# Three chained layers: the fifth attention tile's place in the order, and the weight steps and first split of the last slab

## The chip, the cores and the metric

The kernel runs on one core of a Trainium2 chip. The metric is the device time of one execution in microseconds (us), as the median of several runs. The engines are TensorE (PE, matmuls and transposes), VectorE (DVE), ScalarE (ACT), GpSimd (POOL) and SyncE (SP), which issues the DMAs. Each engine takes its own list of instructions in order.

## The reference

Three layers in a row, on 8 sequences of 576 tokens. Attention over chunks of 64 (8 heads of 64), a layer norm and a feed-forward block of 512 to 2048 to 512 with a residual, and a gated block with a convolution over 3 tokens:

```python
attn = softmax(q_c @ k_c.T / sqrt(64)) @ v_c          # per chunk of 64 tokens and head
x = attn, heads side by side                          # 4608 tokens x 512
xn = (x - mean(x)) / sqrt(var(x) + 1e-6) * g_ln
x2 = x + relu(xn @ w_ch1) @ w_ch2
h = relu(x2 @ w_in)
c = conv3(h, conv_w)                                  # per channel, over 3 tokens of the sequence
out = (h / (1 + exp(-c))) @ w_out
```

## The kernel before

**Precision.** Every fp32 matmul is three passes (L114 to L116, `mm3`): both operands are split in a high and a low part, high by a ScalarE copy, low by a VectorE subtraction. The weights arrive as 64-bit numbers. Turning a piece of 128 x 512 into fp32 takes a step of ScalarE (a, L134) and three of VectorE (t, m and n: L140, L146, L152); for w_ch1 a scaling by g_ln (g), sums (s), and the high and low parts (h, l) come after.

**Stages.** The 4608 tokens are 36 tiles T of 128, and 9 slabs p of 512. In the first stage, for each slab, x @ w_ch1 is computed by a scheme of Strassen's kind: 7 products per quarter G of the columns, 28 slots per slab. A product is 12 matmuls 128x256; its operands are sums of weight blocks and of token blocks (j, u, v make them for a slab). Products 1, 6, 7 and 4 are copied from their bank in PSUM by ScalarE (u1, u6, u7 and u4, L606 and L615), VectorE adds, and the result goes to `hd` in DRAM. Blocks 0 and 1 of the weights (pieces 0 to 7) are the first half of the columns (G = 0, 1), blocks 2 and 3 (pieces 8 to 15) the second. Next is the down phase: for each slab 16 pieces f, each 12 matmuls 128x512. `hr` is reloaded from `hd`, `split` makes hh (ScalarE, relu) and hl (VectorE), `down` multiplies by w_ch2. Then comes the gate phase (w_in, convolution, tanh, w_out).

**Attention inside the first stage.** A tile T has the steps L (load of q, k, v), S (scores on TensorE), M (maximum, VectorE), E (8 exponentials, ScalarE), R (reciprocals, VectorE), P (transposes, TensorE), C (copy, ScalarE), V (values, TensorE), X (scaling on VectorE, store of xd), B (statistics), y (xn), z (transposes), e (copy to bst). What runs ahead of slab 0 is written by hand in the table START: one step after another, W0 to W15 being loads of weight pieces and L0 to L5 of tiles. Behind the bar come lists for slots 0, 1, 2, ... of slab 0, divided by "/"; each list is run after the product of its slot. Later tiles come in by `session(t, tv)`: V of tile tv, S and M of tile tv + 1, X and the load of tile tv + 2 at slot t, halves of E at t + 1 and t + 2, R, P and C at t + 4. The sessions 4 to 7 have slots of their own in slab 0. All loads and stores go by SyncE's queue, in the order of issue; x has two buffers (`bufs=2`), so the third X waits for the first store of xd.

**The last slab.** In slab 8 the pieces of w_ch2 are brought in by a pipeline: `cv_load(n)` issues n loads, and one `cv_step()` runs a of one piece, the VectorE steps of the next older one, and the high and low parts of older ones, then loads one more. The first pieces (`F_ORDER[:4]`, tiles wd0 to wd3) go to the pool `dp` from slot (0,5) on; at (2,5) the other 12 are loaded into tiles of the first half's weights, which are free by then. At (3,2) the two first `hr` are loaded. The split of the first f (`parts = down.split(f)` at n == 0) comes behind all of the slab's products:

```python
for n, (p, f) in enumerate(todo):
    if n == 0:
        parts = down.split(f)
    hh, hl = parts
```

**Between down and gate.** The residual sum x2 (xr, L160) is transposed into the tile x2T (L762, two buffers) and stored in `x2d` (L763), four times for each slab. In the loops these four stand at every second f; those of the last slab are run in a row, behind the last matmuls. The gate tiles (i, f) follow on bank 4 + f % 4: matmuls, relu on ScalarE (hb, L882), taps on VectorE (L897), tanh on ScalarE, gt on VectorE.

Of the kernel before, what the change touches and what calls it, by code (L numbers as in the profile page):

```python
# [8 lines left out]
F32 = mybir.dt.float32  # L9
# [6 lines left out]


START = """
W0 W2 L0 W1 W3 L1 W4 W6 W5 L2 W7 L3 W8 W10 L4 W9 W11 W12 W14 W13 W15 L5
a0 t0 m0 n0 a2 t2 g0 m2 h0 n2 l0 g2 S0 M0 a1 t1 E0 m1 n1 t3 a3 P0 R0 g1  # L20
m3 C0 n3 S1 h1 g3 l1 V0 M1 h2 a4 l2 E1 X0 s0 t4 s2 a6 P1 s1 a5 t5 h4 s3
C1 m5 h3 l4 V1 m4 S2 l3 t6 h5 R1 m6 a7 t7 M2 X1 E2 n5 S3 B1 B0 g5 P2 R2
C2 M3 V2 y0 E3 n6 z0 y1 m7 n4 g6 P3 R3 n7 e0 X2 C3 z1 g7 l5 V3 e1 B2 h9
S4 X3 u1 h8 s4 g4 M4 h6 s6 h7 s5 E4 l6 s7 B3 h11 P4 y2 C4 l11 z2 y3 e2 l7
z3 v1 e3 l9 l8 u3 j0 u2 h10 v3 u5 v2 l10 v5 h12 j1 l12 u7 j2 h13 v7 u6 j3 l13
u4 v6 v4 R4
|
a8 t8 a10 t10 m8 n8
/ g8 a9 t9 m10 n10
/ g10 a11 a12 t11 t12 m9  # L30
/ a14 n9 t14 g9 m12
/ h14 n12 m11 g12 n11 a13
/ l14 t13 g11 m14 h15
/ n14 s8 g14 l15 a15
# [11 lines left out]
def attn_moe_moe2(  # L46
# [34 lines left out]
    NF1 = w_ch1.shape[1] // 128  # L81
# [131 lines left out]
    def cv_load(n=1):  # L213
        for _ in range(n):
            if pieces:
                p = pieces.pop(0)()
                p.load()
                stages[0].append(p)

    def cv_step():  # L220

        now = [s.pop(0) if s else None for s in stages]
        if now[2]:
            now[2].h()
        if now[0]:
            now[0].a()
        if now[1]:
            now[1].m()
        if now[3]:
            now[3].l()  # L230
        for s, p in zip(stages[1:], now):
            if p:
                s.append(p)
        cv_load()
# [21 lines left out]
    def add_w2(f, pool, tag):  # L256
        add(rows(w_ch2, f), w2, f, pool, tag)
# [261 lines left out]
    with tc.manual_schedule():  # L519
# [145 lines left out]
        for tv in range(4, NTILE):  # L665

            t = 28 * (tv // 4 - 1) + 7 * (tv % 4 - 1) + 1
            session({4: 1, 5: 8, 6: 12, 7: 16}.get(tv, t), tv)

        class Down:  # L670

# [21 lines left out]
            def down(self, f, hh, hl):  # L693
                for i in range(4):
                    s = slice(i * 128, (i + 1) * 128)
                    mm3(self.acc[i], hh[:, s], hl[:, s], w2[f][:, 0, :], w2[f][:, 1, :],
                        f == 0, f == NF1 - 1)

        F_ORDER = [f + 8 * i for f in range(8) for i in range(2)]
        dp = None  # L700
        for p in range(NS + 1):
            if p + 1 < NS:
                slabs[p + 1] = Slab(p + 1)
            for G in range(4):
                for s, (n, lag) in enumerate(SLOTS):
                    t = 28 * p + 7 * G + s
                    pp, GG = (p, G - lag) if G >= lag else (p - 1, 3)
                    if 0 <= pp < NS:
                        product(pp, GG, n)
                        nxt = slabs.get(pp + 1)  # L710
                        if GG == 3 and nxt:
                            if n == 1:
                                nxt.j(0)
                                nxt.j(1)
                            nxt.both(n)
                    for fn in events.pop(t, ()):
                        fn()
                    if p == 0 and t < len(later):
                        for step in later[t]:
                            one(step)  # L720
                    if p == NS - 1:
                        if (G, s) == (0, 5):
                            at.p.release()
                            dp = tc.alloc_tile_pool(name="dp", bufs=1, reuse_waits="tile")
                            for i, f in enumerate(F_ORDER[:4]):
                                add_w2(f, lambda: dp, f"wd{i}")
                            cv_load(2)
                        elif (G, s) == (2, 5):
                            tags = [f"w0{kk}{i}" for kk in range(2) for i in range(7)]
                            for f, tag in zip(F_ORDER[4:], tags):  # L730
                                add_w2(f, lambda: wa_p, tag)
                            cv_load(12)
                        elif (G, s) > (0, 5) and s % 2 == 0:
                            cv_step()
                        if (G, s) == (3, 2):
                            down = Down(0)
                            for f in range(2):
                                down.load(f)


        su_p.release()
# [14 lines left out]
        def finish(down, xr):  # L756
            for i in range(4):
                plus(xr[i], down.acc[i], xr[i])
            for i in range(4):
                def store(T=down.T[i], x=xr[i]):  # L760
                    x2T = dp.tile([128, 512], F32, tag="x2T", bufs=2, name="x2T")
                    nc.vector.transpose(out=x2T, in_=x)  # L762
                    nc.sync.dma_start(out=x2d[T].rearrange("p g t -> p (g t)"), in_=x2T)  # L763
                late.append(store)
# [24 lines left out]
        xb = [x_parts(pbx, "xb0")]  # L789
        todo = [(p, f) for p in range(NS) for f in F_ORDER]  # L790
        downs = {0: down}
        xrs = {}
        for n, (p, f) in enumerate(todo):
            if n == 0:
                parts = down.split(f)
            hh, hl = parts

            if f < 8:
                ahead = p * 8 + f + 2
                if ahead < 8 * NS:  # L800
                    if ahead % 8 == 0:
                        downs[ahead // 8] = Down(ahead // 8)
                    downs[ahead // 8].load(ahead % 8)
            if n + 1 < len(todo):
                parts = downs[todo[n + 1][0]].split(todo[n + 1][1])
            if p == 0 and n % 4 < 3 or n % 2:
                cv_step()
            if f == 4:
                xrs[p] = residual(downs[p])
            if late and f >= 8:  # L810
                late.pop(0)()
            downs[p].down(f, hh, hl)
            if f == NF1 - 1:
                finish(downs[p], xrs[p])
            if (p, f) == (0, 15):
                cv_rest()
                load_cw()
                wb_tags = [(wb_p, f"w1{kk}{i}") for kk in range(2) for i in range(7)]
                wb_tags += [(pbx, "wx0"), (pbx, "wx1")]
                for i in range(16):  # L820
                    pool, tag = wb_tags[i]
                    if i < 8:
                        add_wi(i // 4, i % 4, lambda pool=pool: pool, tag)
                    else:
                        add_wo(i - 8, lambda pool=pool: pool, tag)
                cv_load(4)
            if (p, f) == (6, 0):
                load_x2(0)
            if p == 6 and f in (8, 9, 10, 11):
                split_x2(0, f - 8)  # L830
# [182 lines left out]
```

## Time and profile before

| | before |
|---|---|
| median of 3 runs | 1318.85 us (1318.01 to 1320.35) |
| profiled execution, own time | 1322.7 us |
| its span | 1320.8 us |
| TensorE busy | 1247.7 us (94%) |
| VectorE busy | 749.0 us (57%) |
| ScalarE busy | 615.6 us (47%) |
| matmuls | 9096 |

The chain of work that ended last is 88% TensorE, 5% DMA and 4% VectorE. The page gives the span in 40 slices of 33 us: TensorE's busy share is low in the first three or four slices and once again in the fifteenth and sixteenth, the passage from the first stage to the down phase; else it is over 90%. A row of a timeline has the start, the duration, the engine, the line, the operation and the tile, and in brackets for how long the engine had been idle ahead of it and what it waited for.

### The profile page before, as it was taken

What the parts mean: (1) busy time and instruction counts of PE and PEld (TensorE: products, weight loads), DVE (VectorE), ACT (ScalarE), POOL (GpSimd) and SP (SyncE); (2) the same over time, 40 slices, a digit from 0 to 9 for tenths busy, and PEclk for the clock granted to TensorE, in tenths of its full rate; (3) what the DMA queues carried; (4) which work ended last, traced back from release to release, by engine and by line L of the source; (5) the groups of instructions that cost most, each with busy time, mean ns of one, the idle gap of its engine ahead of it and who ended that gap; (6) DMA issues with size and microseconds to landing.
All of it is one profiled execution on the core that took longest, in us unless ns stands there. A gap on an engine that the chain in (4) does not pass through costs nothing.

```text
span 1320.8 us, 23297 instructions
## 1 busy us (share of the span) xinstructions
PE 1247.7 (94%) x9096; PEld 1088.2 (82%) x9096; DVE 749.0 (57%) x1430; ACT 615.6 (47%) x1510; POOL 75.1 (6%) x172
## 2 busy tenths in 40 slices
PE   5468999999999996999999999999999999999998
PEld 4367999999999995787888888888888888888887
DVE  6597565565566455757743333433886555655550
ACT  6575565555565443433422223222675555555541
POOL 0000000000000000000000000000121111111000
PEclk6588999999999998999999999999999999999999
DMA  9523555545554348376543456443111011101001
GB/s 259 171 87 123 192 184 176 178 172 190 185 186 166 131 160 326 120 236 231 196 159 120 149 178 196 132 135 112 48 57 56 25 56 57 56 25 56 25 24 48
DMA packets 127021, 177.70 MB, mean 135 GB/s; under 512 B 12736, under 2 KB 72128, under 8 KB 126912
## 3 DMA queue, kind: packets, MB, share of 16 engines
q1 hardware_dynamic: 126912, 176.22, 40.2%
q8 instruction: 71, 1.16, 0.4%
q14 instruction: 38, 0.31, 0.1%
HBM read 110.13 MB, written 66.06 MB: 133 GB/s over the span
## 4 chain that ended last, share of the span: by engine, by line
PE 88%; DMA 5%; DVE 4%; ACT 2%; SPq 0%; issue 0%; POOL 0%; DVEq 0%; ACTq 0%; POOLq 0%
PE banks L114 28%; PE banks L115 27%; PE banks L116 27%; DMA w<-in_moe_w_ch_dram 2%; PE banks L381 2%; PE banks L463 1%; DMA rq<-in_q_dram 1%; PE banks L421 1%; DVE w L157 1%; DMA hr<-hd 1%; DMA xd<-x 1%; DMA wd<-in_moe_w_ch_dram 0%; DVE xr L160 0%; ACT pp L407 0%; ACT w L336 0%
## 5 line engine op out<-in xcount | busy, mean ns | idle before, releaser
L114 PE MATMUL banks<-xc,w 128*128 128x256 f32 x1008 | 289.9, 288 | 6.6 <-ACT u L606 5.8
L115 PE MATMUL banks<-xc,w 128*128 128x256 f32 x1008 | 282.6, 280 | 0.6 <-DVE xc L157 0.6
L116 PE MATMUL banks<-xc,w 128*128 128x256 f32 x1008 | 282.1, 280 | 0.0
L686 ACT ACTIVATE hh<-hr 128x512 fp32r<-128x512 f32 x144 | 90.9, 632 | 279.0 <-PE banks L116 269.5
L687 DVE SCALAR_TENSOR_TENSOR hl<-hr,hh 128x512 fp32r<-128x512 f32 x144 | 99.2, 690 | 204.9 <-ACT hh L686 204.9
L114 PEld LDWEIGHTS banks<-xc,w 128*128 128x128 f32 x1008 | 192.5, 191 | 10.0 <-ACT u L606 6.5
L115 PEld LDWEIGHTS banks<-xc,w 128*128 128x128 f32 x1008 | 192.9, 191 | 0.8 <-DVE xc L157 0.8
L116 PEld LDWEIGHTS banks<-xc,w 128*128 128x128 f32 x1008 | 192.7, 191 | 0.0
L114 PE MATMUL banks<-w,hl 128*128 128x512 f32 x432 | 168.5, 390 | 0.0
L115 PE MATMUL banks<-w,hh 128*128 128x512 f32 x432 | 168.1, 389 | 0.0
L116 PE MATMUL banks<-w,hh 128*128 128x512 f32 x432 | 168.1, 389 | 0.0
L897 DVE SCALAR_TENSOR_TENSOR cv<-hb,cw_sb,cv 128x510 f32<-128x510 f32 (+31 forms) x256 | 117.3, 513 | 0.6
L115 PE MATMUL banks<-xb,w 128*128 128x512 f32 x288 | 113.0, 392 | 0.0
L114 PE MATMUL banks<-xb,w 128*128 128x512 f32 x288 | 112.9, 392 | 0.0
L116 PE MATMUL banks<-xb,w 128*128 128x512 f32 x288 | 112.8, 392 | 0.0
L160 DVE TENSOR_TENSOR u<-banks,u 128x512 f32<-128x512 f32 x108 | 73.6, 689 | 60.0 <-ACT u L606 32.8
L114 PEld LDWEIGHTS banks<-w,hl 128*128 128x128 f32 x432 | 81.1, 188 | 18.3 <-DVE hl L687 1.4
L116 PEld LDWEIGHTS banks<-w,hh 128*128 128x128 f32 x432 | 81.1, 188 | 17.0
L115 PEld LDWEIGHTS banks<-w,hh 128*128 128x128 f32 x432 | 81.1, 188 | 16.5
L606 ACT COPY u<-banks 128x512 f32<-128x512 f32 x108 | 64.0, 593 | 59.9 <-PE banks L116 56.8
L407 ACT ACTIVATE pp<-banks,mx 128x64 f32<-128x64 f32 x288 | 87.7, 333 | 3.3 <-DVE mx L398 2.8
L115 PE MATMUL banks<-w,Gh 128*128 128x512 f32 x216 | 84.3, 390 | 0.0
(106 smaller groups left out, 2095.0 us busy)
## 6 DMA issues: line engine op xcount, KB each, us to landing
hd<-u SPq DMA_DIRECT2D x144, 256.0 KB, 3.0
hr<-hd SPq DMA_DIRECT2D x72, 512.0 KB, 4.1
w<-in_moe_w_ch_dram SPq DMA_DIRECT2D x28, 512.0 KB, 7.6
rv<-in_v_dram SPq DMA_DIRECT2D x36, 256.0 KB, 4.0
xd<-x SPq DMA_DIRECT2D x36, 256.0 KB, 2.0
xr<-xd SPq DMA_DIRECT2D x36, 256.0 KB, 5.1
x2d<-x2T SPq DMA_DIRECT2D x36, 256.0 KB, 2.1
x2r<-x2d SPq DMA_DIRECT2D x36, 256.0 KB, 4.1
```

What stands on the lines that cost most here:

```text
L114: nc.tensor.matmul(ps, ll, rh, start=first, stop=False, **kw)
L115: nc.tensor.matmul(ps, lh, rl, start=False, stop=False, **kw)
L116: nc.tensor.matmul(ps, lh, rh, start=False, stop=last, **kw)
L157: nc.vector.tensor_tensor(out=out, in0=a, in1=b, op=ALU.subtract)
L160: nc.vector.tensor_tensor(out=out, in0=a, in1=b, op=ALU.add)
L381: nc.tensor.matmul(ps[half(c), e, j, :], lt[half(e), j, c, :], rt[half(e), j, c, :], start=True, stop=True,)
L407: nc.scalar.activation(out=pp[:, j, e, :], in_=self.both[T][:, e, j, :], func=AF.Exp, scale=SCALE, bias=mx[:, e, j:j + 1], accum_out=sm[:, ...
L421: nc.tensor.transpose(tp[:, j * 128:(j + 1) * 128], pp[:, j].rearrange("p e k -> p (e k)"), ident)
L606: nc.scalar.copy(flat(t), bank[to])
L686: nc.scalar.activation(out=self.hh, in_=t, func=AF.Relu)
L687: nc.vector.scalar_tensor_tensor(out=self.hl, in0=t, scalar=0.0, in1=self.hh.bitcast(F32), op0=ALU.max, op1=ALU.subtract,)
L897: nc.vector.scalar_tensor_tensor(out=cv[:, a:e], in0=hb[:, a + tap:e + tap], scalar=cw_sb[:, tap, f:f + 1], in1=cv[:, a:e], op0=ALU.mult, ...
```

## The change

Three things. (1) START: the fifth tile's load L4 now comes ahead of W8, the first load of the second half's weights. Its steps S4, M4 and E4 stand in slot 0's list of slab 0, R4 and P4 in slot 2's, C4 in slot 3's. The other steps ahead of the bar are the same, in another order. The sessions 4, 5, 6 and 7 move from slots 1, 8, 12 and 16 to 5, 9, 13 and 17. (2) Slab 8: five pieces of w_ch2 instead of four are loaded early (a tile wd4 is new), eleven instead of twelve at (2,5). The weight steps behind (2,5) stand at (3,1), (3,3) and (3,5); they stood at (2,6), (3,0), (3,2), (3,4) and (3,6). The split of the first f is made at (3,4). (3) x2T has one buffer.

```diff
 START = """
-W0 W2 L0 W1 W3 L1 W4 W6 W5 L2 W7 L3 W8 W10 L4 W9 W11 W12 W14 W13 W15 L5
+W0 W2 L0 W1 W3 L1 W4 W6 W5 L2 W7 L3 L4 W8 W10 W9 W11 W12 W14 W13 W15 L5
...
-a8 t8 a10 t10 m8 n8
+S4 M4 E4 a8 t8 a10 t10 m8 n8
...
-            session({4: 1, 5: 8, 6: 12, 7: 16}.get(tv, t), tv)
+            session({4: 5, 5: 9, 6: 13, 7: 17}.get(tv, t), tv)
...
+        EARLY = 5
...
-                            for i, f in enumerate(F_ORDER[:4]):
+                            for i, f in enumerate(F_ORDER[:EARLY]):
...
-                            for f, tag in zip(F_ORDER[4:], tags):
+                            for f, tag in zip(F_ORDER[EARLY:], tags):
                                 add_w2(f, lambda: wa_p, tag)
-                            cv_load(12)
-                        elif (G, s) > (0, 5) and s % 2 == 0:
+                            cv_load(NF1)
+                        elif (0, 5) < (G, s) < (2, 5) and s % 2 == 0 or (G, s) in ((3, 1), (3, 3), (3, 5)):
                             cv_step()
...
+                        if (G, s) == (3, 4):
+                            parts = down.split(0)
...
-                    x2T = dp.tile([128, 512], F32, tag="x2T", bufs=2, name="x2T")
+                    x2T = dp.tile([128, 512], F32, tag="x2T", bufs=1, name="x2T")
...
-            if n == 0:
-                parts = down.split(f)
```

ScalarE, from the copy u1 of slab 0's first product on. w1_ are tiles of the second half's weights: L134 (L133 in the changed kernel) is step a, L311 (L310) step g, the copies L606 (L605) take products out of their banks, pp are the exponentials E. Before:

```order
L606 COPY u1_749<-banks_171 128x512
L134 ACTIVATE w1_751<-w1_263 128x512
L134 ACTIVATE w1_754<-w1_265 128x512
L311 ACTIVATE w1_751<-w1_751,g_sb_173 128x512
L134 ACTIVATE w1_751<-w1_275 128x512
L407 ACTIVATE pp_823,sm_822<-banks_171,mx_803 128x64 x4
```

and now:

```order
L605 COPY u1_712<-banks_171 128x512
L406 ACTIVATE pp_734,sm_733<-banks_171,mx_730 128x64 x8
L133 ACTIVATE w1_743<-w1_271 128x512
L133 ACTIVATE w1_746<-w1_273 128x512
L310 ACTIVATE w1_743<-w1_743,g_sb_173 128x512
```

The eight exponentials of tile 4 stand between u1 and the first step a of the second half's weights; before, that step came right behind u1, and the next exponentials (of tile 5, four) four steps later.

ScalarE, around the first hh of the down phase. u7 and u4 are the copies of the last quarter's products 7 and 4, cy and w00n are the pipeline of w_ch2. Before:

```order
L606 COPY u7_7063<-banks_171 128x512
L188 CAST w002_7067<-cy_6992 128x512
L134 ACTIVATE cy_7069<-w004_6910 128x512
L615 COPY u4_7087<-banks_171 128x512
L686 ACTIVATE hh_7113<-hr_6997 128x512
L686 ACTIVATE hh_7119<-hr_6997 128x512
L188 CAST w003_7123<-cy_7031 128x512
```

and now:

```order
L685 ACTIVATE hh_7030<-hr_6993 128x512
L187 CAST w000_7048<-cy_6976 128x512
L133 ACTIVATE cy_7050<-w002_6916 128x512
L605 COPY u7_7067<-banks_171 128x512
L614 COPY u4_7083<-banks_171 128x512
L685 ACTIVATE hh_7111<-hr_6993 128x512
L187 CAST w001_7115<-cy_7011 128x512
```

The first hh moved from behind u4 to ahead of u7, with a weight step between.

VectorE, behind the last slab's down matmuls: the four transposes into x2T, an operand of the gate phase (xb, L111 or L110) and the first taps (cv, L897); in brackets what an instruction waits for, DMAHW being DMAs. Before:

```order
L762 STREAM_TRANSPOSE x2T_9994<-xr_9862 128x512 [waits DVE_49]
L762 STREAM_TRANSPOSE x2T_9997<-xr_9862 128x512 [waits DMAHW1_49,DVE_49]
L762 STREAM_TRANSPOSE x2T_10000<-xr_9865 128x512 [waits DMAHW0_49,DVE_49]
L762 STREAM_TRANSPOSE x2T_10003<-xr_9865 128x512 [waits DMAHW1_49,DVE_49]
L111 TENSOR_TENSOR xb12_10029<-x2r_9263,xb10_10027 128x512 [waits Activation_49]
L897 SCALAR_TENSOR_TENSOR cv_10044<-hb_10043,cw_sb_174,cv_10044 128x510
```

and now:

```order
L764 STREAM_TRANSPOSE x2T_9994<-xr_9862 128x512 [waits DMAHW1_49,DVE_49]
L764 STREAM_TRANSPOSE x2T_9997<-xr_9862 128x512 [waits DMAHW0_49,DVE_49]
L764 STREAM_TRANSPOSE x2T_10000<-xr_9865 128x512 [waits DMAHW1_49,DVE_49]
L764 STREAM_TRANSPOSE x2T_10003<-xr_9865 128x512 [waits DMAHW2_49,DVE_49]
L110 TENSOR_TENSOR xb12_10029<-x2r_9263,xb10_10027 128x512 [waits Activation_49]
L897 SCALAR_TENSOR_TENSOR cv_10044<-hb_10043,cw_sb_174,cv_10044 128x510
```

With one buffer, every transpose waits for the DMA of the one right ahead of it; before, for the one ahead of that.

## Rows read from the trace of the kernel before

**Rows 1.** Stretch, length, busy PE, PEld, DVE, ACT, POOL (instructions), PEclk, DMA share, GB/s.

```profile
51.30:115.80 64.50, 38.94 (x440) 35.67 (x440) 58.46 (x116) 42.84 (x124) 3.65 (x5) 0.79 0.26 83
...
474.00:525.30 51.30, 37.84 (x289) 36.32 (x288) 28.35 (x47) 19.23 (x34) 0.00 (x0) 0.87 0.78 276
```

**Rows 2.** Timeline of VectorE, start: start us, us, engine line operation out<-in count [idle<-releaser].

```profile
51.32 0.69 DVE L435 TENSOR_TENSOR x<-banks,sm 128x512 f32<-128x512 f32 x1 [12.72 <-DMA xd<-x]
...
72.08 0.68 DVE L146 SCALAR_TENSOR_TENSOR w<-w,w 128x512 int32<-128x512 int32 x1
...
87.99 0.44 DVE L140 TENSOR_SCALAR w<-w 128x512 int32<-128x512 uint32 x1
...
88.33 0.68 DVE L157 TENSOR_TENSOR w<-w,w 128x512 f32<-128x512 f32 x1
...
104.29 0.65 DVE L397 TENSOR_REDUCE mx<-banks 128x8 f32<-128x512 f32 x1
...
113.09 0.69 DVE L157 TENSOR_TENSOR w<-s,w 128x512 fp32r<-128x512 f32 x1 [0.68 <-ACT w L336]
```

**Rows 3.** Timeline of ScalarE: weight step, first and last of eight E activates.

```profile
70.44 1.23 ACT L134 ACTIVATE w<-w 128x512 f32<-128x512 f32 x2
...
120.63 0.32 ACT L407 ACTIVATE pp<-banks,mx 128x64 f32<-128x64 f32 x1
...
122.67 0.36 ACT L407 ACTIVATE pp<-banks,mx 128x64 f32<-128x64 f32 x1
```

**Rows 4.** Timeline of TensorE, start: P6 and V7.

```profile
97.76 0.66 PE L421 MATMUL banks<-ident,pp 128*128 128x128 f32 x4 [3.32 <-ACT pp L407]
...
115.83 0.95 PE L381 MATMUL banks<-rv,pt 64*64 64x64 f32 x32 [0.24 <-ACT pt L427]
```

**Rows 5.** Timeline of TensorE in slab 8: products, then the first down matmul.

```profile
503.17 0.39 PE L114 MATMUL banks<-xc,w 128*128 128x256 f32 x1 [1.65 <-ACT u L606]
...
504.65 0.28 PE L114 MATMUL banks<-xc,w 128*128 128x256 f32 x1
...
521.76 0.80 PE L114 MATMUL banks<-wd,hl 128*128 128x512 f32 x1 [9.19 <-DVE hl L687]
```

**Rows 6.** Timeline of SyncE's DMA issues in slab 8.

```profile
497.25 9.25 SPq L125 DMA_DIRECT2D w<-in_moe_w_ch_dram  x12
...
510.01 1.84 SPq L680 DMA_DIRECT2D hr<-hd  x2
```

**Rows 7.** Timeline of ScalarE: first hh.

```profile
520.36 1.15 ACT L686 ACTIVATE hh<-hr 128x512 fp32r<-128x512 f32 x2 [8.51 <-DMA hr<-hd]
```

**Rows 8.** Busy time by stretch, inside TensorE's wait and just behind it.

```profile
515.00:520.00 5.00, 0.00 (x0) 0.00 (x0) 0.00 (x0) 0.00 (x0) 0.00 (x0) 0.55 1.03 353
521.76:525.34 3.58, 3.58 (x8) 2.81 (x9) 2.88 (x5) 0.84 (x2) 0.00 (x0) 0.50 1.07 374
```

**Rows 9.** Timeline of VectorE in the down phase: two hl in a row.

```profile
539.29 0.69 DVE L687 SCALAR_TENSOR_TENSOR hl<-hr,hh 128x512 fp32r<-128x512 f32 x1
...
542.29 0.69 DVE L687 SCALAR_TENSOR_TENSOR hl<-hr,hh 128x512 fp32r<-128x512 f32 x1
```

**Rows 10.** The tile x2T: a wait of ScalarE (us, times), and its stores' landing.

```profile
  ACT cv L886: 0.9, 1
...
DMA to landing us min/median/max: 2.0/2.1/3.4
```

**Rows 11.** Timeline of VectorE: last transposes x2T, before the gate phase.

```profile
920.63 1.29 DVE L762 STREAM_TRANSPOSE x2T<-xr 128x512 f32<-128x512 f32 x2
...
923.47 1.37 DVE L762 STREAM_TRANSPOSE x2T<-xr 128x512 f32<-128x512 f32 x2 [1.55 <-DMA x2d<-x2T]
```

**Rows 12.** Timeline of ScalarE: relu of gate tile (0,7).

```profile
948.69 0.59 ACT L882 ACTIVATE hb<-banks 128x512 f32<-128x512 f32 x1
```

**Rows 13.** Timeline of TensorE: first matmul of gate tile (1,3).

```profile
950.40 0.39 PE L114 MATMUL banks<-xb,w 128*128 128x512 f32 x1
```

**Rows 14.** DMA issues of the page: operation, count, KB each, median us to landing.

```profile
hr<-hd SPq DMA_DIRECT2D x72, 512.0 KB, 4.1
```

More of the change, by code (lines that the diff above doesn't have):

```diff
@@ L18 @@
 START = """
-W0 W2 L0 W1 W3 L1 W4 W6 W5 L2 W7 L3 W8 W10 L4 W9 W11 W12 W14 W13 W15 L5
+W0 W2 L0 W1 W3 L1 W4 W6 W5 L2 W7 L3 L4 W8 W10 W9 W11 W12 W14 W13 W15 L5
 a0 t0 m0 n0 a2 t2 g0 m2 h0 n2 l0 g2 S0 M0 a1 t1 E0 m1 n1 t3 a3 P0 R0 g1
[L21 to L26, printed above, removed]
+m3 C0 n3 S1 h1 g3 l1 V0 M1 h2 a4 t4 E1 X0 s0 t6 s2 a6 s1 P1 a5 t5 s3 h4
+R1 h3 m6 C1 l2 m5 V1 B0 S2 X1 a7 t7 M2 m7 E2 n5 l3 S3 n6 m4 g5 P2 M3 g6
+C2 n4 E3 V2 l4 n7 B1 h5 R2 P3 R3 g7 y0 l5 C3 z0 y1 h9 V3 X2 e0 l9 g4 z1
+X3 h8 h7 B2 e1 B3 h6 u1 l7 v1 y3 l8 z3 s4 e3 y2 s6 z2 s5 e2 l6 h11 j0 u2
+j1 u3 s7 u5 v3 u7 h10 l11 j2 l10 u6 v2 h12 v6 j3 l12 u4 v5 h13 v4 l13 v7
 |
-a8 t8 a10 t10 m8 n8
+S4 M4 E4 a8 t8 a10 t10 m8 n8
 / g8 a9 t9 m10 n10
-/ g10 a11 a12 t11 t12 m9
-/ a14 n9 t14 g9 m12
+/ g10 a11 a12 t11 t12 m9 R4 P4
+/ C4 a14 n9 t14 g9 m12
 / h14 n12 m11 g12 n11 a13
```

## The prediction

> **What bounds the kernel now.** I first read the table of stretches [rows 1]. From 51.30 to 115.80 us TensorE is busy for 38.94 of 64.50 us at a granted clock of 0.79, and VectorE for 58.46: here VectorE sets the pace. From 474.00 to 525.30 us TensorE is busy for 37.84 of 51.30. Everywhere else TensorE is busy nearly all the time, at full clock. So an edit counts where it moves the time at which TensorE comes out of these two holes, or where it opens a third. The change touches both, and, by one buffer, the passage to the gate phase.
>
> **The start.** The first number to fix is where the stretch begins: the fill's loads stand ahead of the xd stores on SyncE, and VectorE's third scaling X2 waits 12.72 us for a store, until 51.32 [rows 2]. L4 only changes places with weight loads, the sum of bytes ahead of the stores is the same, so X2 stays there; the earlier L4 buys nothing.
>
> From there I walk VectorE's list. S4, M4 and E4 now stand after the first product, behind the slab splits, so the last xc subtraction comes about 0.9 us sooner (M4 and its scaling are no longer ahead of it). But M4 must then run, and ScalarE does the eight E activates, which take 2.4 us (120.63 to 123.03 in a row of them, [rows 3]), ahead of a8, which took 0.6 us each in a pair [rows 3]. VectorE's first m step of the second-half weights needs a8; it ran at 72.08 [rows 2] and now comes at 69.0 (last xc) + 0.6 + 0.85 (M4) + 2.4 + 0.6 + 0.1 = 73.6, an estimate: +1.5 us, all of it VectorE idle. VectorE is idle for only 6.04 of the stretch's 64.50 us [rows 1], so little slack is left to take this back.
>
> Next, the sessions. Before, session 4 stood at slot 1 and session 5 at slot 8, seven slots apart; now 5 and 9. A session hands on a chain: E on ScalarE, P on TensorE, C on ScalarE, V and S on TensorE, M on VectorE. With four slots between, this chain is bare. Before, sessions that stood four apart show it: P6 began at 97.76 after 3.32 us of waiting for ScalarE, and the reduction M7 at 104.29, so from P to M it is 6.5 us [rows 2, 4]. In the new order, 27 VectorE instructions (12 scalar_tensor_tensor, 4 tensor_tensor, 5 tensor_scalar, a statistics one, 5 small) stand between the first m step and the last n step of piece 14. At the spacing of these kinds (about 0.65, 0.60 and 0.34 us between starts, by the rows from 72.08 and 87.99 on; the statistics 0.7, small ones 0.15) that is 14 us [rows 2], so it ends at 87.7. Behind it on ScalarE stand a g, an a, a copy and half an E, 3 us, so P5 begins at 90.7 and M6 at 97.3, where VectorE's own list is ready at 93.9: a new wait of 3.4 us. After M6 come 20 tensor_tensor, 4 others and 8 small ones before the last weight subtraction, 16.8 us with the waits between; it begins at about 114.1, where it began at 113.09 before [rows 2], and the statistics of session 6 (1.0 us) now fall behind it. TensorE then has P7 at 117.5 and V7 at 118.7, where V7 stood at 115.83 [rows 4]. V7 now stands behind one product more (slot 17 instead of 16), worth about 1.4 us (12 matmuls from 503.17 to 504.65, the first one slow; [rows 5]). So **the start costs 118.7 - 115.83 - 1.4 = +1.5 us**. The cost is worked out from a list, not read, so its bounds are wide: -2, if M6's wait is covered by work I have put behind it, to +4, if the idle 1.5 and 3.4 both reach the end and nothing of before's waits goes.
>
> **Slab 8.** The hole is a wait for data. SyncE issues twelve weight loads from 497.25, then two stores and at 510.01 the two hr loads [rows 6]; the first hh begins at 520.36 on hr's landing, after 8.51 us of idle time [rows 7], 10.3 us after the issue; meanwhile the DMA engines are full and move 353 GB/s [rows 8]. The load stands at the end of a queue of bytes. TensorE, out of products at 512.57, waits 9.19 us, until 521.76 [rows 5], and then runs at a granted clock of 0.50 until 525.34 [rows 8], which loses it 1.8 us.
>
> Taken one by one: (a) The stalls that the moved weight steps take away (1.65 us before 503.17, [rows 5], and a smaller one) are worth nothing, because TensorE then only comes sooner to the wait for hr. (b) One of twelve weight loads goes into the early group. 0.524 MB less in the queue at 353 to 374 GB/s [rows 8] are 1.4 us: hr lands at 518.95. That is a gain. (c) The first split now stands at slot (3,4), three places ahead of the end of the slab in ScalarE's list and VectorE's. Both engines take their list in order, so the first hh, which waits for hr, now holds up the copies u7 and u4 and VectorE's two sums behind it. The last two products can't begin before u7's copy has freed its bank. What TensorE did during the wait for hr it now does after it: hh ends at 519.6, a weight cast and step, then u7's copy at 521.3; product 4 from 521.35 at half clock to 523.9; product 3 to 525.75; then the first f of the down phase. Before, that f began at 521.76, at half clock, as good as 523.55 at full. So +2.2. (d) One weight step fewer runs ahead of the down phase, one more in it. Where a step runs beside an f, VectorE needs 3.00 us for one f (539.29 to 542.29, [rows 9]) against the 2.7 of TensorE's twelve matmuls (twice the width of a product's, so twice the 1.4), so one more costs at most 0.3; I take 0.1, since the first f's leave VectorE some room. What (b) gives is inside (c)'s times. **Slab 8: +2.3 us**, from 0 (hr lands 2.3 us sooner than I have it, at 516.7) to +4 (no gain from (b), one step more in the way).
>
> **The passage to the gate phase.** The buffers of x2T go from two to one. In the loops one transpose stands at every second f, some 5.4 us (two of 2.7) apart, and a store lands in 2.0 to 2.1 us (worst 3.4, [rows 10]), so nothing waits. But after the last slab four transposes stand back to back. Before, the third waited 1.55 us for the first store: pairs at 920.63 and 923.47, free at 924.8 [rows 11]. That is 2.84 us from a transpose to the one that takes its buffer. Now each takes the buffer of the one ahead: 920.63, 923.47, 926.31, 929.15, VectorE free at 929.8, **5.0 us later**. Behind the transposes in its list stand the taps of the first gate tile, and with them ScalarE's tanh and later relus. One wait of 0.9 us that ScalarE had on the way for such a store [rows 10] goes: 4.1 left. TensorE reuses a bank of the gate phase after four tiles, so the delay meets it at tile (1,3): its bank's relu began at 948.69 and took 0.59 [rows 12], so it was free at 949.3, and TensorE began there at 950.40 [rows 13]: 1.1 us of slack. **Gate: 4.1 - 1.1 = +3.0 us**, from 2.0 (landings at the lower end, some list order kinder) to 5.0 (nothing of it hidden). After that the output tile from 953 us on gives 5.5 us of matmuls that need no relu, so the loss isn't repeated.
>
> Here the Trainium skill gives another size (DMA: Bandwidth & Descriptors, Anatomy of one DMA): a fixed 2.0 us and the bytes at 436 GB/s, on the software path that the page measures. By it a store of 256 KB takes 2.6 us, an estimate, 0.5 to 0.6 over the landing in the row, and three waits would make the gate's term about 4.6. The rows are of these very stores, so the sum goes by them.
>
> **Sum.** 1.5 + 2.3 + 3.0 = +6.8 us. The profiled execution took 1322.7 us with a span of 1320.8; the median of the runs, 1318.85, is 3.85 under it. On the median: **1325.7 us** (a profile of the changed kernel would then show a span near 1327.6).
>
> **Rivals.** First, the x2T wait is hidden: the list of VectorE slips by 5 us, but gate tiles queue with more slack than the one pair of rows shows, or the first output tile comes in time. For: TensorE's loops have no wait before 950. Against: 1.1 us of slack is read directly. It gives +3.8: 1322.7.
> Second, start and slab 8 come out even (start -1, slab 0, gate +2.5): M6 is covered and the last products meet an hr that lands 2 us sooner. It gives 1320.4, within 0.2% of before (2.6 us, about what a measurement of this kernel can tell from no change).
> Third, on the other side: hr is not behind the bytes. If its landing depends on when it is issued and on what share of the engines it gets (over all 72 hr loads the median is 4.1 us, [rows 14]), TensorE, rid of 2.3 us of stalls, would issue hr 2 us sooner, find it landed by the split and run straight from the last product into the down phase, at about 510.3 and at full clock. In the forecast the down phase begins 6.8 us after hr's landing (518.95 to 525.75), so it decides from a landing of about 512 (519.05 less 6.8): there the 4.5 us of the other terms are paid. With hr there by 507 the hole is gone: 510.3 instead of 523.55 is -13.25, of which the start and the gate take 4.5: 1310.1. Against it: 353 GB/s and a landing of 10.3 us say the queue was full.
> Fourth, worse: both waits at the start reach the end, no stall goes in slab 8, and nothing hides the gate's: +4 +4 +5 = 1331.9.
>
> **How the numbers follow.** Forecast (1322.5 to 1329.5): 0.57. x2T hidden: 0.12. Even: 0.13. hr early: 0.12, which includes milder gains. Worse: 0.06. The range goes from 1318.5, which takes in the even case, to 1330.0; it leaves out the early hr and most of the worse case, 0.18. Faster 0.12, same 0.14, slower 0.74.
>
> **What would show it.** Start: VectorE's idle time ahead of the first m step and of M6, and V7 at about 118.7 with a product more ahead of it. If V7 stands under 117, the walk was wrong. Slab 8: hh at about 519 with the wait for hr in ScalarE's list, the copy of u7 right behind it, two products and only then the down phase near 525.7. If the products ran on ahead of hr, (c) is wrong; if hh begins under 512, the queue of bytes is. Gate: four single transposes 2.84 us apart, and TensorE idle for some 3 us near 950. Spacing under 2.3 or no idle time there refutes that term.

## The result, and the profile after

The changed kernel is slower: 1329.11 us (1327.76 to 1330.37, 4 runs) against 1318.51 (1318.01 to 1320.35, 4 runs), a ratio of 1.0078 with an interval of 1.006 to 1.0095, which on 1319 us is +10.3 us (7.9 to 12.5). The forecast was 1325.7, +6.8, in a range of 1318.5 to 1330.0. The direction was right and the time lies in the range; of the size, 3.5 us were missing. The profiled execution took 1329.09 us with a span of 1327.2.

The first stretch after (columns as in [rows 1]):

```profile
51.30:115.80 64.50, 37.62 (x407) 34.70 (x408) 54.31 (x107) 36.28 (x101) 3.20 (x4) 0.69 0.20 66
```

Here TensorE got through 407 matmuls instead of 440, at a clock of 0.69 instead of 0.79, and VectorE is idle for 10.2 us instead of 6.0. VectorE's timeline of the start shows where (start, duration, operation, and in brackets the idle time ahead and its releaser):

```profile
50.75 0.69 DVE L434 TENSOR_TENSOR x<-banks,sm 128x512 f32<-128x512 f32 x1 [12.47 <-DMA xd<-x]
...
73.20 0.69 DVE L145 SCALAR_TENSOR_TENSOR w<-w,w 128x512 int32<-128x512 int32 x1 [2.50 <-ACT w L133]
...
97.05 0.69 DVE L396 TENSOR_REDUCE mx<-banks 128x8 f32<-128x512 f32 x1 [3.54 <-PE banks L380]
...
113.51 0.69 DVE L396 TENSOR_REDUCE mx<-banks 128x8 f32<-128x512 f32 x1 [1.62 <-PE banks L380]
...
117.72 0.69 DVE L156 TENSOR_TENSOR w<-s,w 128x512 fp32r<-128x512 f32 x1 [0.69 <-ACT w L335]
```

These answer to [rows 2]: X2, the first m step of the second half's weights, M6, M7 and the last weight subtraction. The wait for M6 is there as forecast (3.54 us, 3.4 forecast). Ahead of the m step VectorE idles for 2.50 us where the forecast had 1.5; the step itself begins at 73.20, 22.45 us after X2, against 20.76 before. But the last subtraction is at 117.72, not at 114.1. TensorE's tile V of session 6 and of session 7 at the end of this stretch, and that of session 8, which stands in the same slot of slab 1 in both kernels:

```profile
111.39 1.13 PE L380 MATMUL banks<-rv,pt 64*64 64x64 f32 x32 [5.75 <-ACT pt L426]
...
122.05 0.69 PE L380 MATMUL banks<-rv,pt 64*64 64x64 f32 x32 [0.65 <-ACT pt L426]
...
131.70 0.69 PE L380 MATMUL banks<-rv,pt 64*64 64x64 f32 x32
```

Slab 8, ScalarE, SyncE (these answer to [rows 7] and [rows 6]) and then TensorE, the first matmul of the last but one product and the first of the down phase:

```profile
519.51 0.63 ACT L685 ACTIVATE hh<-hr 128x512 fp32r<-128x512 f32 x1 [14.62 <-DMA hr<-hd]
520.04 0.60 ACT L187 CAST w<-cy 128x512 fp32r<-128x512 f32 x1
520.55 0.66 ACT L133 ACTIVATE cy<-w 128x512 f32<-128x512 f32 x1
521.12 0.56 ACT L605 COPY u<-banks 128x512 f32<-128x512 f32 x1
524.70 0.59 ACT L614 COPY u<-banks 128x512 f32<-128x512 f32 x1 [3.02 <-PE banks L115]
```

```profile
497.60 8.68 SPq L124 DMA_DIRECT2D w<-in_moe_w_ch_dram  x11
...
509.85 1.77 SPq L679 DMA_DIRECT2D hr<-hd  x2
```

```profile
521.73 0.58 PE L113 MATMUL banks<-xc,w 128*128 128x256 f32 x1 [14.45 <-ACT u L605]
...
526.38 0.39 PE L113 MATMUL banks<-wd,hl 128*128 128x512 f32 x1
```

ScalarE's wait for hr grew from 8.51 to 14.62 us, and u7's copy, at 521.12, and u4's, at 524.70, now come behind it: the two products ran after hr's landing, and TensorE waited 14.45 us for u7 where it had waited 9.19 for the first hl [rows 5]. The passage to the gate phase on VectorE (these answer to [rows 11]) and TensorE's two longest waits in it:

```profile
923.71 0.70 DVE L764 STREAM_TRANSPOSE x2T<-xr 128x512 f32<-128x512 f32 x1
926.53 0.71 DVE L764 STREAM_TRANSPOSE x2T<-xr 128x512 f32<-128x512 f32 x1 [2.12 <-DMA x2d<-x2T]
929.38 0.71 DVE L764 STREAM_TRANSPOSE x2T<-xr 128x512 f32<-128x512 f32 x1 [2.13 <-DMA x2d<-x2T]
932.20 0.71 DVE L764 STREAM_TRANSPOSE x2T<-xr 128x512 f32<-128x512 f32 x1 [2.12 <-DMA x2d<-x2T]
```

```profile
942.90 0.50 PE L113 MATMUL banks<-xb,w 128*128 128x512 f32 x1 [0.23 <-ACT hb L882]
...
947.16 0.50 PE L113 MATMUL banks<-xb,w 128*128 128x512 f32 x1 [1.19 <-ACT hb L882]
```

The transposes are 2.82 to 2.85 us apart (2.84 forecast). Up to the first of them the changed kernel has lost 923.71 - 920.63 = 3.08 us against the profile of before, and at the end of the span 6.4, so the gate took 3.3.

### The profile page after: what moved, and what is told of

The parts are those of the page before. It is cut to its first block, busy times and chain, and to the rows that moved or that the text cites. A ratio compares the mean times of both kernels' runs of the same rounds, so it can differ in the third digit from the quotient of the medians.

```text
span 1327.2 us, 23315 instructions
## 1 busy us (share of the span) xinstructions
PE 1247.7 (94%) x9096; PEld 1086.4 (82%) x9096; DVE 748.5 (56%) x1430; ACT 614.8 (46%) x1510; POOL 75.2 (6%) x172
## 4 chain that ended last, share of the span: by engine, by line
PE 85%; DVE 5%; DMA 5%; ACT 3%; issue 1%; SPq 1%; POOL 0%; DVEq 0%; ACTq 0%; POOLq 0%
PE banks L113 27%; PE banks L114 27%; PE banks L115 27%; PE banks L380 3%; DMA w<-in_moe_w_ch_dram 2%; PE banks L462 1%; DVE w L156 1%; PE banks L420 1%; DMA hr<-hd 1%; DMA rq<-in_q_dram 1%; DMA xd<-x 0%; DMA x2d<-x2T 0%; ACT pp L406 0%; DVE xr L159 0%; DVE w L151 0%
## 5 line engine op out<-in xcount | busy, mean ns | idle before, releaser
L113 PE MATMUL banks<-w,hl 128*128 128x512 f32 x396 | 154.7, 391 | 0.0
L115 PE MATMUL banks<-w,hh 128*128 128x512 f32 x396 | 154.1, 389 | 0.0
L114 PE MATMUL banks<-w,hh 128*128 128x512 f32 x396 | 154.1, 389 | 0.0
L897 DVE SCALAR_TENSOR_TENSOR cv<-hb,cw_sb,cv 128x510 f32<-128x510 f32 (+31 forms) x256 | 117.1, 512 | 0.6
L605 ACT COPY u<-banks 128x512 f32<-128x512 f32 x108 | 64.0, 593 | 54.0 <-PE banks L115 52.3
L113 PEld LDWEIGHTS banks<-w,hl 128*128 128x128 f32 x396 | 74.3, 188 | 17.2 <-DVE hl L686 2.1
L115 PEld LDWEIGHTS banks<-w,hh 128*128 128x128 f32 x396 | 74.3, 188 | 15.6
L114 PEld LDWEIGHTS banks<-w,hh 128*128 128x128 f32 x396 | 74.3, 188 | 15.3
```

Of the source, the lines that this page charges most:

```text
L113: nc.tensor.matmul(ps, ll, rh, start=first, stop=False, **kw)
L114: nc.tensor.matmul(ps, lh, rl, start=False, stop=False, **kw)
L115: nc.tensor.matmul(ps, lh, rh, start=False, stop=last, **kw)
L605: nc.scalar.copy(flat(t), bank[to])
L897: nc.vector.scalar_tensor_tensor(out=cv[:, a:e], in0=hb[:, a + tap:e + tap], scalar=cw_sb[:, tap, f:f + 1], in1=cv[:, a:e], op0=ALU.mult, ...
```

## The experiments

All ratios are to the kernel before, measured beside each run; us are on 1319.

**The kernel before, a second profile.** No edit.

> The kernel before, once more, for a second profile. The profiled execution of before lay 3.85 us over its median and the one of the changed kernel lay on its median, so the two profiles differ by 6.4 us where the medians differ by 10.6. Theory A (the extra 4 us of that one profile lie in the start, where the stretch to 115.8 us depends on when the xd stores land): the tile V of session 7 stands 3 to 4 us earlier than 115.83 and all later stretches have the same lengths. Theory B (they lie in the down or gate phase): V stands at 115.8 within 0.5. Ratio of times 1.000.

Ratio 1.0005 (0.9994 to 1.0016), span 1318.4. X2 on VectorE, and on TensorE the V of sessions 7 and 8:

```profile
49.22 0.69 DVE L435 TENSOR_TENSOR x<-banks,sm 128x512 f32<-128x512 f32 x1 [12.50 <-DMA xd<-x]
```

```profile
113.71 0.73 PE L381 MATMUL banks<-rv,pt 64*64 64x64 f32 x32 [0.24 <-ACT pt L427]
...
125.81 0.69 PE L381 MATMUL banks<-rv,pt 64*64 64x64 f32 x32
```

Theory A held for the start, with 2.1 us instead of 3 to 4: the first profile was late because X2's wait ended late, and from X2 to V7 both profiles need 64.5 us (115.83 - 51.32, 113.71 - 49.22). So a start is compared from X2 on. From X2 to V8 this profile takes 76.59 us, as the first one does, the changed kernel 131.70 - 50.75 = 80.95: its start costs 4.4. The later stretches aren't all of the same length, as theory A had it: from X2 to the last V, of tile 35, the two profiles of before take 395.87 and 397.16 us.

**The start alone.**

```diff
-            session({4: 1, 5: 8, 6: 12, 7: 16}.get(tv, t), tv)
+            session({4: 5, 5: 9, 6: 13, 7: 17}.get(tv, t), tv)
```

with the new START table; the rest as before.

> The kernel before with the new START table and the sessions at 5, 9, 13, 17, nothing else. Theory (the start costs time by itself: VectorE waits for E4 ahead of the second half's weights and for the bare chain to M6): slower by 3.5 to 8 us (1322 to 1326.5), last weight subtraction near 117.7 against 113.1, hr landing later by the same amount, so that nothing of it is taken back. Rival (the start is neutral and the loss of the whole change lies in slab 8 and the gate): within 1.5 us of before.

Ratio 1.0034 (1.0019 to 1.005), +4.5 us. X2 is at 50.54, the last subtraction at 117.67, V8 at 131.68, 81.14 after X2. On VectorE:

```profile
50.54 0.69 DVE L434 TENSOR_TENSOR x<-banks,sm 128x512 f32<-128x512 f32 x1 [12.29 <-DMA xd<-x]
...
96.84 0.69 DVE L396 TENSOR_REDUCE mx<-banks 128x8 f32<-128x512 f32 x1 [3.54 <-PE banks L380]
...
117.67 0.69 DVE L156 TENSOR_TENSOR w<-s,w 128x512 fp32r<-128x512 f32 x1 [0.69 <-ACT w L335]
```

The rival (a neutral start) falls. The start reproduces by itself what the whole change shows there. At the last V a part of it may be gone again: the four profiles with the change's START and sessions (the changed kernel, this one, and the two on the changed kernel with another slab 8) stand there 398.27 to 400.29 us after X2, the seven with the old START 394.44 to 397.16, the means 3.6 apart.

**One x2T buffer alone.**

```diff
-                    x2T = dp.tile([128, 512], F32, tag="x2T", bufs=2, name="x2T")
+                    x2T = dp.tile([128, 512], F32, tag="x2T", bufs=1, name="x2T")
```

> The kernel before with one x2T buffer instead of two, nothing else. Theory (three transposes wait for the store of the one ahead, 1.1 us of slack hides a part): VectorE idle three times 2.1 us at the passage, time +3.0 to +3.5 us (1321.5 to 1322.0). Rival (the gate phase's slack hides it): the same three waits, and a time within 0.7 us of before.

Ratio 1.0036 (1.0024 to 1.0047), +4.7 us (3.2 to 6.2). In the trace three transposes wait, as in the changed kernel:

```profile
918.74 0.70 DVE L762 STREAM_TRANSPOSE x2T<-xr 128x512 f32<-128x512 f32 x1
921.55 0.71 DVE L762 STREAM_TRANSPOSE x2T<-xr 128x512 f32<-128x512 f32 x1 [2.11 <-DMA x2d<-x2T]
```

The first is 1.89 us sooner than in the first profile of before, and the span of 1322.9 ends 2.1 later: 4.0 us by this one edit. The forecast mechanism stands, the size was somewhat small.

**Slab 8 alone.** The split at (3,4) and the weight steps at (3,1), (3,3), (3,5), with four early pieces and two x2T buffers:

```diff
-                        elif (G, s) > (0, 5) and s % 2 == 0:
+                        elif (0, 5) < (G, s) < (2, 5) and s % 2 == 0 or (G, s) in ((3, 1), (3, 3), (3, 5)):
                             cv_step()
...
+                        if (G, s) == (3, 4):
+                            parts = down.split(0)
```

> The kernel before with slab 8's changes alone: first split at (3,4), weight steps at (3,1), (3,3), (3,5); with four early pieces and two x2T buffers as before. Theory (TensorE's last two products wait behind hr in the lists of ScalarE and VectorE, and the stalls that go make the loads start about 2 us sooner): the first hh ends TensorE's wait, two products behind it, down phase 6.8 us after hr's landing; time -1 to +3 us against before. Rival (the two products run ahead of hr, and what is won is the whole of the stalls): -3 us or more.

Ratio 1.0037 (1.0024 to 1.005), +4.9 us (3.2 to 6.6), more than expected. From the first hh to the first transpose of the last four, a distance with no start in it, the two profiles of before take 400.27 (920.63 - 520.36) and 400.64 us, this kernel 404.58 (918.81 - 514.23), the changed kernel 404.20 (over the six other runs with the old split and hr behind the weights it is 399.85 to 400.61). The first of the four transposes here, on VectorE:

```profile
918.81 1.29 DVE L765 STREAM_TRANSPOSE x2T<-xr 128x512 f32<-128x512 f32 x2
```

Two products of about 1.4 us at full clock stand in that distance, run at a granted clock of 0.54 on the mean from 514.23 to 521.00: +3.9 to +4.3. The gain ahead of it, from the first weight load to hh, is 1.0 us (514.23 - 492.15 = 22.08, against 23.11 before).

**The changed kernel, with the split back behind the products.**

```diff
-                        if (G, s) == (3, 4):
-                            parts = down.split(0)
...
+            if n == 0:
+                parts = down.split(f)
```

> The changed kernel with the first split back behind all products of slab 8, nothing else. Theory (the two last products stood behind hr in the lists of ScalarE and VectorE): both products run before hr lands; hr lands as before, and the down phase begins some 3 us after it instead of 7; time -3 to -4.5 us against the changed kernel (1324.5 to 1326). Rival (the split's place is neutral, because the weight steps are what delays): within 1 us of the changed kernel (1328 to 1330).

Ratio 1.005 (1.003 to 1.007), 1326.11 us, 3.0 under the changed kernel's median and 3.7 by the ratios; the intervals of the two overlap, so the trace decides. hh comes 21.5 us after the first load, the products run before it, and TensorE waits on hl as in [rows 5]:

```profile
519.42 0.79 PE L113 MATMUL banks<-wd,hl 128*128 128x512 f32 x1 [9.04 <-DVE hl L686]
```

From hh (518.01) to the first transpose (918.53) are 400.52 us, as in the kernel before. So all that the changed kernel loses in this distance is due to the place of the split.

**The changed kernel, with hr ahead of the weight loads.**

```diff
                         elif (G, s) == (2, 5):
+                            down = Down(0)
+                            for f in range(2):
+                                down.load(f)
                             tags = [f"w0{kk}{i}" for kk in range(2) for i in range(7)]
...
-                        if (G, s) == (3, 2):
-                            down = Down(0)
-                            for f in range(2):
-                                down.load(f)
```

> The changed kernel with the two hr loads issued at (2,5), ahead of the eleven weight loads, instead of at (3,2) behind them. Theory (hr's landing is set by the bytes queued ahead of it, not by when it is wanted): hr is there some 5 us after its issue, the first hh no longer waits, the down phase starts straight behind the last product, -9 to -14 us against the changed kernel (1315 to 1320), the weights landing 2 to 3 us later. Rival (the weights of the first pieces or the DMA engines themselves are the bound, so that the same wait only moves to the first weight steps): -3 us or less.

Ratio 1.0002 (0.9988 to 1.0016): some 10 us faster than the changed kernel. ScalarE, the first weight step of the second group and the first hh:

```profile
503.78 0.69 ACT L133 ACTIVATE cy<-w 128x512 f32<-128x512 f32 x1 [6.56 <-DMA w<-in_moe_w_ch_dram]
...
505.89 0.63 ACT L685 ACTIVATE hh<-hr 128x512 fp32r<-128x512 f32 x1
```

hh waits for nothing. The same two loads, issued at 495.09 instead of behind eleven others, were there by their turn. The waits of TensorE from 470 to 600 us (us in total, times, longest), in the changed kernel and here:

```profile
PE banks L113 <- ACT u L605: 15.7, 2, 14.5
...
PE banks L113 <- ACT u L605: 4.4, 3, 2.1
```

This is the place and the sign of the forecast's third rival, reached by an edit that the change doesn't contain.

**The kernel before, with the same edit.** The two hr loads at (2,5), ahead of the twelve weight loads.

> The kernel before with the same edit: the two hr loads issued at (2,5), ahead of the twelve weight loads. Theory: TensorE's wait of 9.2 us for hr goes; the weight steps at (2,6) to (3,6) wait 2 to 3 us longer for their loads and hold up the copies behind them; -5 to -10 us against before (1309 to 1314). Rival (the wait only moves to the weight loads): -2 us or less.

Ratio 0.9973 (0.996 to 0.9986), -3.6 us (-5.3 to -1.8), less than expected. ScalarE's first weight step at (2,6) and TensorE behind it:

```profile
504.57 0.68 ACT L134 ACTIVATE cy<-w 128x512 f32<-128x512 f32 x1 [8.99 <-DMA w<-in_moe_w_ch_dram]
```

```profile
505.77 0.58 PE L114 MATMUL banks<-xc,w 128*128 128x256 f32 x1 [6.74 <-ACT u L606]
```

The wait of 9.19 us for hr fell to 1.43, but the one behind the weight steps grew from 1.65 [rows 5] to 6.74: where the step stands as early as in the kernel before, most of the won time (5.1 of 7.8 us) is lost to the next load in the queue.

**Both: the change's places in slab 8, and hr ahead of the weights.** The edits of the two runs on slab 8 (split and steps, hr first) on the kernel before.

> The kernel before with the change's slab-8 places (split at (3,4), weight steps at (3,1), (3,3), (3,5)) and the two hr loads issued at (2,5) ahead of the twelve weight loads; START, four early pieces and two x2T buffers as before. Theory: with hr there in time the early split costs nothing and the weight steps' waits are shorter than in the kernel before with hr first; -8 to -12 us against before (1307 to 1311), faster than both kernels. Rival (the weight steps' waits for their loads now bound the slab): no better than the kernel before with hr first.

Ratio 0.9965 (0.9953 to 0.9977), 1313.93 us, -4.6: faster than both kernels, short of what was expected. The times don't tell it from the kernel before with hr first (0.996 to 0.9986); in the traces it is 2.9 us shorter from X2 to the end (1261.76, 1264.66). TensorE waits again, later, for the third hr:

```profile
522.09 0.63 ACT L686 ACTIVATE hh<-hr 128x512 fp32r<-128x512 f32 x1 [5.47 <-DMA hr<-hd]
```

```profile
523.50 0.80 PE L114 MATMUL banks<-w,hl 128*128 128x512 f32 x1 [3.42 <-DVE hl L687]
```

**Three hr loads ahead of the weights.** The kernel of the run ahead, with

```diff
-                            for f in range(2):
+                            for f in range(3):
                                 down.load(f)
...
-                if ahead < 8 * NS:
+                if 2 < ahead < 8 * NS:
```

> The kernel before with the first split at (3,4), weight steps at (3,1), (3,3), (3,5), and three instead of two hr loads at (2,5), ahead of the twelve weight loads. Theory (with two, the third hr stood behind the weights' bytes again: ScalarE waited 5.5 us for it and TensorE 3.4): both waits go, the weights land another 1.4 us later; 2 to 3.5 us faster than with two, 1310 to 1312. Rival (the bytes only change places: the weight steps wait as much longer): within 1 us of the run with two.

Ratio 0.9954 (0.994 to 0.9969), 1313.17 us, -6.1, the fastest kernel here. Less was won over the kernel with two than the 2 to 3.5 us expected. The waits of TensorE from 470 to 600 us are down to one kind:

```profile
PE banks L114 <- ACT u L606: 5.5, 3, 3.0
```

The wait for the third hr is gone, and the one behind the weight steps is 3.0 us instead of 2.1 at its longest. The span is 1.4 us shorter than with two (1310.4, 1311.8); the intervals of the two overlap, so that it is faster than with two is not shown by the times.

**E4 later.** The start alone, with

```diff
-S4 M4 E4 a8 t8 a10 t10 m8 n8
+S4 M4 a8 t8 a10 t10 m8 n8 E4
```

> The kernel before with the new START and sessions (as in the run of the start alone, +4.5 us), but with E4 behind n8 at the end of slot 0's list. Theory (VectorE's idle 2.5 us ahead of the first m step of the second half's weights is due to E4 standing ahead of a8 on ScalarE, and it goes through to the end): that idle time falls under 0.5 us and the last weight subtraction and V of session 7 come 1.5 to 2.5 us sooner after X2 than with the start alone; +2 to +3.5 us against before. Rival (the later waits for M6 and M7 swallow it): within 1 us of the start alone.

Ratio 1.0024 (1.001 to 1.0038), +3.2 us. On VectorE the first m step no longer waits, and M6 waits just as long, so the whole rest moved up:

```profile
72.62 0.69 DVE L145 SCALAR_TENSOR_TENSOR w<-w,w 128x512 int32<-128x512 int32 x1
...
96.46 0.69 DVE L396 TENSOR_REDUCE mx<-banks 128x8 f32<-128x512 f32 x1 [3.54 <-PE banks L380]
```

X2 was at 52.75 here. M6 stands 43.71 us after it instead of 46.30, and V8 78.51 instead of 81.14: 2.6 us, the whole idle time of the start alone (2.49).

**Session 4 one slot sooner.** The start alone, with

```diff
-            session({4: 5, 5: 9, 6: 13, 7: 17}.get(tv, t), tv)
+            session({4: 4, 5: 9, 6: 13, 7: 17}.get(tv, t), tv)
```

> The kernel before with the new START, session 4 at slot 4 instead of 5, the others at 9, 13, 17. Theory (E5 stands too close ahead of P5: the chain E, P, C, V, S, M is bare, and M6 waits 3.5 us): P5 no longer waits for E, M6's wait falls under 1.5 us, V of session 7 comes 1 to 2.5 us sooner than with the start alone; +2 to +3.5 us against before. Rival (M6 waits for its slot's products, not for E5): the wait for M6 stays above 2.5 us and the time within 1 us of the start alone.

Ratio 1.0022 (1.0011 to 1.0032), +2.9 us. P5 on TensorE and then M6 on VectorE:

```profile
87.97 0.66 PE L420 MATMUL banks<-ident,pp 128*128 128x128 f32 x4 [1.07 <-ACT pp L406]
```

```profile
94.39 0.69 DVE L396 TENSOR_REDUCE mx<-banks 128x8 f32<-128x512 f32 x1
```

M6's wait is gone and P5's fell from 3.94 to 1.07; a wait of 1.94 for M5, at 80.83, is new. V8 stands 78.76 us after X2 (50.28), 2.4 sooner than with the start alone.

**All four sessions one slot sooner.** The start alone, with slots 4, 8, 12 and 16.

> The kernel before with the new START, sessions at 4, 8, 12, 16: the three later ones where they stood before. Theory (the last of the forecast's missing 3 us is M7, which in the changed kernel stands ahead of the last weight subtractions in VectorE's list and waits 1.6 us there; one slot earlier it waits less, or more, by where P6's E stands): last subtraction 1 to 3 us sooner than with the start alone; +1.5 to +3.5 us against before. Rival (the slots of the later sessions don't matter, the loss is E4 and M4 behind the bar): within 1 us of the start alone.

Ratio 1.0031 (1.0017 to 1.0045), +4.1 us. On VectorE M6 and the last subtraction:

```profile
94.36 0.69 DVE L396 TENSOR_REDUCE mx<-banks 128x8 f32<-128x512 f32 x1 [0.69 <-PE banks L380]
...
116.70 0.69 DVE L156 TENSOR_TENSOR w<-s,w 128x512 fp32r<-128x512 f32 x1 [0.68 <-ACT w L335]
```

X2 was at 50.62. The last subtraction stands 66.08 us after it against 67.13 with the start alone, the lower end of what the theory had, V8 80.55 against 81.14. M7's wait is gone and M6's fell to 0.69, but waits of 1.95 for M5 and 1.13 for a cast are new. By the times the rival holds within its microsecond: where sessions 5 to 7 stand is worth little as long as they keep four slots between them; the fifth slot between 4 and 5 (78.76 to V8, against 80.55 here) is what pays.

## Why the prediction was right, and where it was too small

**The start, +1.5 forecast, +4.4 measured (trace, at V8) and +4.5 (2.5 to 6.6; the start alone).** Three of the forecast's steps came out to a few tenths: X2 stays within the spread of the profiles, the first m step comes 1.7 us later (1.5 forecast), and the chain between sessions 4 and 5 is bare, so that M6 waits 3.54 at 97.05. The step that failed is the next one, "After M6 come 20 tensor_tensor, 4 others and 8 small ones before the last weight subtraction", 16.8 us; measured are 20.67 (97.05 to 117.72). VectorE's list has five others there: m, n, a statistics one, xn and M7, which stands ahead of the last three weight subtractions. M7 waited 1.62 us for TensorE and took 0.8 with its scaling, 2.4 of the 3.9 us that are missing. The last two subtractions waited 0.74 and 0.69 for casts, as they did before (0.74 and 0.68); whether the forecast's 16.8 has these waits in it, it doesn't say. TensorE was late for M7 because V6 waited 5.75 us for the copy C6.

Of the two causes, each is shown in the trace by an edit of its own: E4's place is worth 2.6 us, the fifth slot 2.4 (by the times +3.2 and +2.9 remain of +4.5, which their intervals don't part). So both idle times reach the end, the case that the forecast had at its upper bound, +4. Whether both edits together would win the sum wasn't tried.

**Slab 8, +2.3 forecast, +4.9 (3.2 to 6.6) alone.** The run alone keeps all twelve loads, so (b) isn't in it; without (b)'s 1.4 the forecast would be +3.7, inside the interval. (a) was right in kind: with its earlier stalls gone TensorE only came sooner to a longer wait. (c) was right in mechanism and size: the down phase began 6.87 us after hh (519.51 to 526.38), 6.8 forecast. That is 3.6 us more than the 3.2 from [rows 7] to 523.55; up to the transposes 3.6 to 3.9 are measured against the two profiles of before, and moving the split back removes all of it. (b) came out in the changed kernel. From the first weight load to hh (columns as in [rows 1]) in the kernel before, the changed kernel, the one with the split moved back, and slab 8 alone:

```profile
497.25:520.36 23.11, 13.00 (x110) 12.41 (x108) 11.37 (x19) 7.86 (x15) 0.00 (x0) 0.89 0.95 348
...
497.60:519.51 21.91, 9.68 (x86) 9.48 (x84) 3.11 (x5) 3.42 (x7) 0.00 (x0) 0.83 0.94 345
...
496.48:518.01 21.53, 13.23 (x111) 12.82 (x109) 6.90 (x11) 5.74 (x10) 0.00 (x0) 0.89 0.94 346
...
492.15:514.23 22.08, 9.71 (x86) 9.51 (x84) 3.19 (x5) 3.58 (x6) 0.00 (x0) 0.83 0.98 368
```

With eleven loads hh came 1.2 and 1.6 us sooner at the rate of before (345 and 346 GB/s against 348), around the 1.4 of the forecast: what came was fewer bytes, 7.56 MB in the changed kernel (21.91 us at 345 GB/s) against 8.04. The seven profiles with twelve loads and the old places take 22.8 to 23.3 us. With twelve, slab 8 alone gained 1.0 in another way: its DMA engines moved 368 GB/s. What raised the rate in that profile stays open. That the queue of bytes sets hr's landing, on which (b) rested, is shown by the runs with hr first.

**The gate, +3.0 forecast, 3.3 in the changed kernel's trace, 4.0 in that of the buffer alone, +4.7 (3.2 to 6.2) by its times.** The spacing, VectorE's delay and the sum were right. ScalarE's second cv step and the relu of (0,7) in the changed kernel, and that cv step in the run of the buffer alone:

```profile
929.34 0.72 ACT L886 ACTIVATE cv<-hb,cw_sb 128x511 f32<-128x511 f32 x1
...
955.97 0.59 ACT L882 ACTIVATE hb<-banks 128x512 f32<-128x512 f32 x1
...
930.12 0.72 ACT L886 ACTIVATE cv<-hb,cw_sb 128x511 f32<-128x511 f32 x1 [5.78 <-DVE cv L897]
```

In the changed kernel this relu begins 32.26 us after the first transpose (955.97 - 923.71), before it was 28.06 [rows 11, 12]: 4.2 later, 4.1 forecast. Less the 1.1 us of slack at tile (1,3) that is 3.1, and TensorE began (1,3) 3.1 later (32.91 after the first transpose against 29.77). It waited from (0,7) on, but less, for the slack was larger there: the tiles (0,7), (1,0), (1,1) and (1,2) began 0.4, 1.9, 2.3 and 2.7 later. With the buffer alone the cv step waits for VectorE's taps, the relus come 4.9 later, and the gate costs 4.0; why it ran ahead of the taps only in the changed kernel isn't shown. The Trainium skill's fit for a store (DMA: Bandwidth & Descriptors, Anatomy of one DMA), measured on the path of GpSimd's DMAs, makes 2.6 us of these 256 KB, an estimate, and 4.6 of the term. For these stores, issued by SyncE, it isn't borne out: half of them landed within 2.1 us here too, and the waits are 2.12.

**The sum.** The three parts alone add up to 14.1 us, the whole is 10.3. Slab 8 alone lacks (b), which takes back 1.2 in the changed kernel, and the gate cost 0.7 less there than alone. The half-widths of the four intervals (2.0, 1.5, 1.7 and 2.3), combined as independent, make 3.8, so that the rest is no difference. Stretch by stretch the traces give 3.6 to 4.4 for the start, -1.2 and +3.6 to +3.9 for slab 8 and 3.3 for the gate, 9.3 to 10.4. The first two profiles by themselves show less, 6.9 us from X2 to the end (1276.42 against 1269.50): from the last V to slab 8's first weight load before's took 50.06 us and the changed kernel's 47.65, on a way that takes 47.65 to 50.13 over the ten profiles with hr behind the weights. So the forecast's 6.8 was short by the 2 to 3 us of the start for the most part. That its span of 1327.6 met the measured 1327.2 is luck: before's profile lay 3.85 us over its median, the changed kernel's on its own.

**The rivals.** x2T hidden: no. Start and slab 8 even: no, both cost. hr early: not in the change, but in the run with hr first. It brought 10 us against the changed kernel, where the forecast's two times (1325.7 and 1310.1) are 15.6 apart: TensorE still waits 4.4 us there for copies out of the banks, and ScalarE, ahead of them, 6.56 for the first weights. Worse: of its three terms only the start's came in the changed kernel.

## What to carry to other kernels

An instruction moved ahead in an engine's list takes its wait with it: put a step that waits for a transfer behind everything that doesn't need it, or bring the transfer forward first. A wait at the end of a long queue of loads is shortened by the order of the issues, not by asking sooner; then look at what stands next in that queue, for it will wait instead. In a stage set by a chain across three engines, count every link of it in the other engine's list, the last one too.

## What the hardware showed

A fill of the same bytes ends at different times: over the fourteen profiles of this case X2's wait ended between 47.85 and 52.75 us, and the start behind it moved along (from X2 to V8 the seven profiles with the old START take 76.09 to 77.40 us). A difference of one or two microseconds between two profiles of the whole is not a reading before that has been taken out, and the way from the last V to slab 8's first weight load adds as much again.
